# A two-layer mixture of experts on one core: VectorE's word for a count ahead of two weight conversions, and ten operations of the experts' order behind the second pair of tiles

## The chip, the cores and the metric

The kernel runs on one core of one Trainium2 chip. A core has five engines that run their own instruction streams: TensorE (PE in the profile), VectorE (DVE), ScalarE (ACT), GpSimd (POOL) and SyncE (SP), which here issues nearly all transfers. They meet through semaphores. The metric is the time of one execution on the device, in microseconds (us); less is better.

## The reference

The input is q, k, v for 8 batches, 8 heads, 576 positions of width 64. A retention (a causal attention with a decay for each head instead of a softmax) gives a matrix x of 4608 tokens by 512. Two mixture-of-experts layers follow, each with 8 experts and one expert for each token:

```
logits = x @ w_gate                      # layer 2: + modality_bias[modality_id]
e_idx  = argmax(logits, axis=1)          # one expert of 8 for each token
gate_w = softmax(logits)[e_idx]
for e in range(8):
    h        = max(x[mask_e] @ w1[e], 0) # 512 -> 1024
    out[mask_e] = gate_w * (h @ w2[e])   # 1024 -> 512; layer 1: * sigmoid(x @ w_output_gate)[e]
```

The output is the second layer's out, 4608 by 512, in float32.

## The kernel before, in words

**Stages.** In the first 190 us the attention is computed, each token is routed, and its row is scattered to the place of its expert in a buffer in DRAM (xs1). Then come 16 positions: position P_ 0 to 7 is an expert of layer 1, 8 to 15 one of layer 2 (E is 8). Layer 1's results go through the second gate on the way and are scattered to a second buffer (xs2), sorted by their next expert. The experts of layer 2 are taken in an order by size, which is not known before the tokens of layer 1 are counted.

**A position.** An expert's tokens are worked in pairs of tiles of 128 (a pair is 256 rows, `unit(P_, 0, PAIR)` and `unit(P_, 1, PAIR)`), and what is left over in a third block of 128 rows or fewer (`unit(P_, 2, FULL)`). In this run position 6 has two pairs and a third block. In a unit TensorE first makes four quarters of the hidden layer (lines 999 to 1001). ScalarE writes the maximum with zero in float16 (L1101) and VectorE what float16 left out of it (L1213); both are needed by the second product (lines 1007 to 1009), first for the tile b=0, then for b=1. ScalarE and VectorE then cut each result tile to a row of the next layer (`back`, lines 1086 and 1177), the last operation being an x2row.

**Routing of results lags behind.** The rows of a finished unit are transposed by SyncE (x2T, L806), in `turn_next`, which stands in SyncE's `unit` for the unit after next: the rows of the second pair of expert 6 are turned in SyncE's unit for the first pair of expert 7, behind the transpose of that pair's own rows (xT, L820). TensorE makes their second-layer logits (L977, in `logits`) between its other matmuls one unit later than the unit that made them: those of the second pair of expert 6, tile 0, in the middle of the third block's second product. VectorE chooses the expert (`choose`), TensorE counts the rank (`ranks`, L982), VectorE makes the place (`place`), GpSimd scatters.

**Weights.** SyncE loads the next expert's weights in four quarters of 1 MB (stg, L791, `next_w`); ScalarE (L1078) and VectorE (`conv`, L1145) convert a quarter each to two float16 parts. VectorE does two of these conversions at the end of a first pair (line 1222), one in the second pair, one at its end. The slot of a quarter is free again (stg_free) after VectorE's conversion.

**The order of layer 2.** At the end of the first pair of position 6 (`asked`, line 744: P_ is E-2, slot 0), VectorE gives the word `cnt_ask`. TensorE's `counts` (L986) takes it, and with it pr_free1, the slot that VectorE's `place` frees, at the end of its unit, and sums the counts of the eight experts over the partitions (L988). VectorE's `order` (L1237) takes the result (cnt_full), subtracts, and makes the order by ten more operations on 8 or 64 elements of one partition. It ends with four words: ord_sp, ord_pe, ord_ac and ord_po. TensorE, ScalarE and GpSimd take theirs ahead of position 7. SyncE takes ord_sp in `next_w` (line 795) ahead of the first load of position 8's weights, and it issues that load at the end of position 6 (line 924), behind all of position 6's transfers and ahead of all of position 7's. SyncE's instructions, like those of the other engines, run in program order, so what stands behind a wait waits too.

All operations of VectorE's chains go through a helper and so carry its line, L477; they are told apart by their tiles (r_cf is the subtraction's result, wb a converted weight, oh the chosen expert, x2row a result's row).

Of the kernel before, what the change touches and what calls it, by code (L numbers as in the profile page):

```python
# [20 lines left out]
D, F, E = 512, 1024, 8  # L21
# [470 lines left out]
def experts(nc, st, I, K, out):  # L492
# [37 lines left out]
    T = Take(nc)  # L530
# [5 lines left out]
    def cols(P_, w):  # L536

        return slice(0, w) if w != SMALL or P_ < E else slice(P - w, P)
# [26 lines left out]
    def when(eng, reg, op, val):  # L565
        return eng.If_cmp(reg, val, f"IS_{op}")
# [48 lines left out]
    def entered(eng, R_, P_):  # L615

        if P_ < E + 2:
            return ExitStack()
        return when(eng, R_["left"][P_ - E], "GT", 0)
# [24 lines left out]
    def pairs_from(eng, R_, P_, unit, k):  # L644

        pairs, i = R_["np"][P_ % E], R_["i"]
        eng.reg_mov(i, k)
        with eng.While(lambda: eng.snap(i) < eng.snap(pairs)):
            unit(P_, 0, PAIR, True)
            eng.reg_add(i, i, 1)  # L650
            with eng.If(eng.snap(i) < eng.snap(pairs)):
                unit(P_, 1, PAIR, True)
                eng.reg_add(i, i, 1)

    def walk(co, R_, P_, unit, none=None, conv=None, first=None):

        eng, pairs, od = co.eng, R_["np"][P_ % E], R_["od"][P_ % E]
        if P_ < E:
            block, after = co.label("block"), co.label("after")

            def without():
                if none:
                    none()
                if first and P_ == 0:
                    first()
                for q in range(2 if conv and P_ == 0 else 0):
                    conv(0, 2 + q)
                if conv:
                    for slot in range(2):
                        for q in range(2):  # L670
                            brought(eng, R_, P_, conv, slot, q)

            def other():
                with when(eng, pairs, "GT", 1):
                    unit(P_, 1, PAIR, True, 1)
                    pairs_from(eng, R_, P_, unit, 2)
                if conv:
                    with eng.Else():
                        for q in range(2):
                            brought(eng, R_, P_, conv, 1, q)  # L680
            co.unlikely(pairs, "LT", 1, without, block)
            unit(P_, 0, PAIR, False, 0)
            co.unlikely(pairs, "NE", 2, other, block)
            unit(P_, 1, PAIR, True, 1)
            co.to(block)
            co.jump(od, "EQ", 0, after)
            unit(P_, 2, FULL, False)
            co.to(after)
            return
        with when(eng, pairs, "GT", 0):  # L690
            unit(P_, 0, PAIR, False, 0)
            with when(eng, pairs, "GT", 1):
                unit(P_, 1, PAIR, True, 1)
                pairs_from(eng, R_, P_, unit, 2)
        if none:
            with eng.Else():
                none()
        with when(eng, od, "EQ", 2):
            unit(P_, 2, FULL, False)
        with eng.Else():  # L700
            with when(eng, od, "EQ", 1):
                unit(P_, 2, SMALL, False)
        if conv:
            rest(eng, R_, P_, conv)

    def brought(eng, R_, P_, conv, slot, q):

        if P_ + 1 < NP and None not in (slot, q):
            with entered(eng, R_, P_ + 1):
                conv(P_ + 1, 2 * slot + q)  # L710

    def rest(eng, R_, P_, conv):

        with when(eng, R_["np"][P_ % E], "LT", 2):
            with when(eng, R_["np"][P_ % E], "LT", 1):
                for q in range(2):
                    brought(eng, R_, P_, conv, 0, q)
            for q in range(2):
                brought(eng, R_, P_, conv, 1, q)
# [13 lines left out]
    def behind(P_, slot):  # L733

        return P_ < E and (P_, slot) != (0, 0)
# [8 lines left out]
    def asked(P_, slot):  # L744

        return P_ == E - 2 and slot == 0
# [16 lines left out]
    with nc.Block() as block:  # L763
# [374 lines left out]
        def _(ve):  # L1138
            ch = Chain(ve, T, "dve")
            tt, ts, stt, tr = ve.tensor_tensor, ve.tensor_scalar, ve.scalar_tensor_tensor, ve.tensor_reduce  # L1140
            with ExitStack() as rs:
                R_ = registers(rs, ve, "ve", ("i", "was", "early"))
# [63 lines left out]
                def unit(P_, s, w, sure, slot=None, routing=None):  # L1206
                    cs = cols(P_, w)
                    for g in range(4):
                        routes = routing or behind(P_, slot)
                        if routes and g < 3:  # L1210
                            routed(ve, was, s, sure, g, choose, 2)
                        take(ve, "hh_full")
                        stt(hT[:, 1, 2 * g:2 * g + 2, cs], ph[g][:, :, cs], 0.0, hT[:, 0, 2 * g:2 * g + 2, cs], op0=ALU.max, op1=ALU.subtract).then_inc(T["h_full"])  # L1213
                        if routes:
                            if g == 3:
                                routed(ve, was, s, sure, g, choose, 2)
                            routed(ve, was, s, sure, g, place, 2)
                        if P_ == 0 and slot == 0 and g < 2:
                            conv(0, 2 + g)
                        if slot == 1 and g == 1:  # L1220
                            brought(ve, R_, P_, conv, slot, 0)
                    for q in range(2 - (slot or 0)):
                        brought(ve, R_, P_, conv, slot, q + (slot or 0))
                    if routing or asked(P_, slot):
                        ve.sem_inc(T["cnt_ask"])
                    for b in range(blocks[s]):
                        back(s, b) if P_ < E else final(s, b)
                    if asked(P_, slot):
                        order()
                    if P_ < E:  # L1230
                        note(ve, was, s, sure)
# [2 lines left out]
                over = lambda a: a.unsqueeze(1).to_broadcast([1, E, E])  # L1234
                along = lambda a: a.unsqueeze(2).to_broadcast([1, E, E])

                def order():  # L1237

                    take(ve, "cnt_full")
                    ch(tt, r8["cf"], pk[0:1], col("eP")[0:1], op=ALU.subtract)  # L1240
                    ch.tell("pr_free1")
                    ch(stt, r8["key"], r8["cf"], 8.0, col("desc")[0:1], op0=ALU.mult, op1=ALU.add)
                    ch(tt, r64["cmp"], over(r8["key"]), along(r8["key"]), op=ALU.is_gt)
                    ch(tr, r8["rank"], r64["cmp"], axis=AX.X, op=ALU.add)
                    ch(tt, r64["sel"], over(r8["rank"]), along(e8), op=ALU.is_equal)
                    ch(tt, r64["t"], r64["sel"], over(e8), op=ALU.mult)
                    ch(tr, r8["ord"], r64["t"], axis=AX.X, op=ALU.add)
                    ch(ve.tensor_copy, reg2[:, 0:8], r8["ord"])
                    ch(ts, reg2[:, 32:40], r8["ord"], -1.0, E - 1.0, dep=False, op0=ALU.mult, op1=ALU.add)
                    ch(tr, r8["n2"][:, 0:1], r8["cf"], dep=False, axis=AX.X, op=ALU.max)  # L1250
                    ch(ts, reg2[:, 40:41], r8["n2"][:, 0:1], float(EP * PAIR), None, op0=ALU.is_ge)
                    ch.tell("ord_sp", "ord_pe", "ord_ac", "ord_po")
                    ch.end()
# [27 lines left out]
                co = Course(ve, "ve")  # L1281
# [6 lines left out]
                for P_ in range(NP):  # L1288
                    if P_ == E - 3:
                        ch(ve.tensor_copy, cums, cum)  # L1290
                        ch.end()
                    if P_ == E - 1:
                        learn(ve, R_)
                    if P_ == E:
                        with when(ve, R_["early"], "GT", 0):
                            unit(E, 0, PAIR, False, routing=True)
                            final_counts()
                            unit(E, 1, PAIR, False)
                        with ve.Else():
                            routed(ve, was, 0, False, None, lambda b: (choose(b), place(b)))  # L1300
                            ve.sem_inc(T["cnt_ask"])
                            final_counts()
                        less_early(ve, R_)
                    co.leave(R_, P_)
                    ahead(ve, R_, P_)

                    def none():
                        ve.sem_inc(T["cnt_ask"])
                        order()
                    walk(co, R_, P_, unit, none if P_ == E - 2 else None, conv, nothing)  # L1310
                co.end()

        @block.gpsimd
# [123 lines left out]
```

## Time and profile before

| what | value |
|---|---|
| timed runs | 1017.72, 1019.05, 1019.11 us; median 1019.05 |
| profiled execution, own time | 1011.63 us |
| its span, first to last instruction | 1009.9 us |
| mean granted TensorE clock | 0.986 of full speed |
| bytes moved by DMA | 145.15 MB, mean 144 GB/s |

The profile is of one execution, and the rows below are its. Times in a row are microseconds from the start of the span. A row of a timeline is one instruction, or several alike in sequence (x2): start, duration, engine, line, operation, result<-operands; at the end stands, in brackets, how long the engine was idle before it and what released it (DVEq L465, PEq L465 and the like: the engine's own queue stood at a semaphore wait, which the helper at line 465 issues). Matmuls overlap, so the distance of their starts is what one costs, not its duration. SPq rows are SyncE issuing a transfer; the transfer itself lands later.

### The profile page before, as it was taken

To read this page: it belongs to the slowest core of one execution; us is meant where nothing else is said; L and a number is where in the kernel's file an instruction comes from. 1 tells how busy PE (TensorE), PEld (TensorE's weight loads), DVE (VectorE), ACT (ScalarE), POOL (GpSimd) and SP (SyncE) were. 2 spreads that over 40 slices of the span, in tenths; PEclk is the share of its full clock that TensorE was granted. 3 is DMA by queue.
4 is the path that set the end of the run, shared out by engine and by line. 5 is a ranking of instruction groups with operands and counts; after the bars stand their busy time and mean duration, and the time that the engine had idled before them with its cause. 6 is when DMAs were issued, how large, how long until landed. Compare 5 with 4: busy or idle time off the path is not lost. (4 is left out here: it accounts for less than half of the span.)

```text
span 1009.9 us, 24673 instructions
## 1 busy us (share of the span) xinstructions
PE 972.9 (96%) x8929; PEld 699.1 (69%) x8929; DVE 444.7 (44%) x1395; ACT 352.3 (35%) x693; POOL 232.0 (23%) x301
## 2 busy tenths in 40 slices
PE   8999998499999999999999999999999999999995
PEld 5999997366767677676666667667666667766673
DVE  2566667465655666555656565233111111111111
ACT  3555555352534344444434443133111211111111
POOL 4577666301111121211221121101001101001010
PEclk9999999699999999999999999999999999999998
DMA  8998884587648474839455654551121211122100
GB/s 309 309 315 294 280 305 163 170 243 206 150 140 173 111 201 78 229 77 252 144 146 158 160 149 82 169 120 53 43 63 42 74 34 54 43 52 53 53 31 24
DMA packets 180259, 145.15 MB, mean 144 GB/s; under 512 B 136569, under 2 KB 136733, under 8 KB 180128
## 3 DMA queue, kind: packets, MB, share of 16 engines
q1 hardware_dynamic: 171168, 114.89, 42.3%
q0 software_dynamic: 8960, 28.62, 7.8%
q8 instruction: 70, 1.15, 0.5%
q14 instruction: 61, 0.50, 0.2%
HBM read 80.46 MB, written 33.92 MB: 113 GB/s over the span
## 5 line engine op out<-in xcount | busy, mean ns | idle before, releaser
L999 PE MATMUL ph<-xT,wb 128*128 128x256 f16 (+2 forms) x1344 | 337.2, 262 | 0.1
L1001 PE MATMUL ph<-xT,wb 128*128 128x256 f16 (+2 forms) x1344 | 337.3, 262 | 0.0
L1000 PE MATMUL ph<-xT,wb 128*128 128x256 f16 (+2 forms) x1344 | 337.3, 262 | 0.0
L1213 DVE SCALAR_TENSOR_TENSOR hT<-ph,hT 128x512 f16<-128x512 f32 (+2 forms) x168 | 106.0, 637 | 332.4 <-DVEq L465 331.8
L1009 PE MATMUL py<-wb,hT 128*128 128x512 f16 x608 | 230.4, 379 | 0.0
L1008 PE MATMUL py<-wb,hT 128*128 128x512 f16 x608 | 230.3, 379 | 0.0
L1007 PE MATMUL py<-wb,hT 128*128 128x512 f16 x608 | 230.3, 379 | 0.0
L1101 ACT ACTIVATE hT<-ph 128x512 f16<-128x512 f32 (+2 forms) x168 | 92.4, 551 | 200.7 <-ACTq L465 200.4
L999 PEld LDWEIGHTS ph<-xT,wb 128*128 128x128 f16 x1344 | 131.1, 98 | 16.1 <-issue 0.5
L1000 PEld LDWEIGHTS ph<-xT,wb 128*128 128x128 f16 x1344 | 131.1, 98 | 15.7
L1001 PEld LDWEIGHTS ph<-xT,wb 128*128 128x128 f16 x1344 | 131.1, 98 | 12.4
L1339 POOL DMA_INDIRECT out_dram<-yo,idxo x37 | 36.0, 974 | 335.2 <-POOLq L465 335.2
L1009 PEld LDWEIGHTS py<-wb,hT 128*128 128x128 f16 x608 | 59.4, 98 | 71.8
L1007 PEld LDWEIGHTS py<-wb,hT 128*128 128x128 f16 x608 | 59.3, 98 | 63.4
L1008 PEld LDWEIGHTS py<-wb,hT 128*128 128x128 f16 x608 | 59.4, 98 | 63.2
L1328 POOL TENSOR_SCALAR idx<-v_pos 128x1 int32<-128x1 f32 x39 | 24.4, 625 | 324.9 <-POOLq L465 324.9
L477 DVE SCALAR_TENSOR_TENSOR wb<-stg,wb 128x2048 f16<-128x2048 f32 x38 | 86.9, 2286 | 10.0 <-DVEq L465 9.5
L1095 ACT ACTIVATE yo<-py,v_gcol 128x512 f32<-128x512 f32 x37 | 25.4, 687 | 168.1 <-ACTq L465 168.1
L1078 ACT ACTIVATE wb<-stg 128x2048 f16<-128x2048 f32 x38 | 72.3, 1903 | 1.5 <-ACTq L465 1.3
L1092 ACT ACTIVATE x2row<-py,v_s 128x512 f16<-128x512 f32 x39 | 26.8, 687 | 70.3 <-ACTq L465 70.3
L1332 POOL DMA_INDIRECT xs<-x2row,idx x39 | 42.6, 1093 | 37.8 <-POOLq L465 36.5
L313 ACT ACTIVATE a<-pa 128x512 f32<-128x512 f32 x64 | 34.7, 593 | 38.2 <-PE pa L274 38.0
(152 smaller groups left out, 947.0 us busy)
## 6 DMA issues: line engine op xcount, KB each, us to landing
stg<-in_moe_w_dram SPq DMA_DIRECT2D x38, 1024.0 KB, 7.3
qn<-in_q_dram SPq DMA_DIRECT2D x36, 256.0 KB, 4.1
dkn<-in_dk_dram SPq DMA_DIRECT2D x36, 256.0 KB, 5.1
vn<-in_v_dram SPq DMA_DIRECT2D x36, 256.0 KB, 5.6
kn<-in_k_dram SPq DMA_DIRECT2D x32, 256.0 KB, 5.3
xs<-zero SPq DMA_DIRECT2D x8, 262.0 KB, 2.2
xs<-zero SPq DMA_DIRECT2D x8, 258.0 KB, 3.2
w0s<-in_moe_w_dram SPq DMA_DIRECT2D x8, 256.0 KB, 5.6
```

The lines of the kernel that those rows point to most:

```text
L477: r = fn(*a, **kw).then_inc(self.sem, 1)
L999: pe.matmul(o, w1(P_, 0)[:, c, fs], xT[s][:, c, cs], start=(c == 0), stop=False)
L1000: pe.matmul(o, w1(P_, 0)[:, c, fs], xT[s][:, 4 + c, cs], start=False, stop=False)
L1001: m = pe.matmul(o, w1(P_, 1)[:, c, fs], xT[s][:, c, cs], start=False, stop=(c == 3))
L1007: pe.matmul(py[b], hT[:, 0, f, bs], w2(P_, 0)[:, f, :], start=(f == 0), stop=False)
L1008: pe.matmul(py[b], hT[:, 0, f, bs], w2(P_, 1)[:, f, :], start=False, stop=False)
L1009: m = pe.matmul(py[b], hT[:, 1, f, bs], w2(P_, 0)[:, f, :], start=False, stop=(f == 7))
L1078: ac.activation(wb[P_ % 2][:, 0, 2048 * c:2048 * c + 2048], stg[:, 2048 * c:2048 * c + 2048], AF.Copy, scale=WS).then_inc(T["cv_full"])
L1101: ac.activation(hT[:, 0, 2 * g:2 * g + 2, cs], ph[g][:, :, cs], AF.Relu).then_inc(T["hh_full"])
L1213: stt(hT[:, 1, 2 * g:2 * g + 2, cs], ph[g][:, :, cs], 0.0, hT[:, 0, 2 * g:2 * g + 2, cs], op0=ALU.max, op1=ALU.subtract).then_inc(T["h_full"])
L1332: po.indirect_dma_start(out=xs2, out_offset=bass.IndirectOffsetOnAxis(ap=idx[b], axis=0), in_=x, in_offset=None, bounds_check=E * R - 1, o ...
L1339: po.indirect_dma_start(out=out, out_offset=bass.IndirectOffsetOnAxis(ap=idxo[b], axis=0), in_=yo[b], in_offset=None, bounds_check=N - 1, ...
```

## The change

VectorE's `cnt_ask` in position 6 is given ahead of the two conversions at the end of the first pair instead of behind them. `order` is cut in two: `totals` takes the count, subtracts and frees the slot, where all of `order` stood; the other ten operations and the four words stand at the end of the second pair of the same position. For an expert with one pair or none other branches call them (`late`, `none`); this run doesn't take them.

```diff
+                    if asked(P_, slot):
+                        ve.sem_inc(T["cnt_ask"])
                     for q in range(2 - (slot or 0)):
                         brought(ve, R_, P_, conv, slot, q + (slot or 0))
-                    if routing or asked(P_, slot):
+                    if routing:
                         ve.sem_inc(T["cnt_ask"])
                     for b in range(blocks[s]):
                         back(s, b) if P_ < E else final(s, b)
                     if asked(P_, slot):
+                        totals()
+                    if (P_, slot) == (E - 2, 1):
                         order()
...
-                def order():
+                def totals():
 
                     take(ve, "cnt_full")
                     ch(tt, r8["cf"], pk[0:1], col("eP")[0:1], op=ALU.subtract)
                     ch.tell("pr_free1")
+                    ch.end()
+
+                def order():
+
                     ch(stt, r8["key"], r8["cf"], 8.0, col("desc")[0:1], op0=ALU.mult, op1=ALU.add)
...
                     def none():
                         ve.sem_inc(T["cnt_ask"])
+                        totals()
                         order()
-                    walk(co, R_, P_, unit, none if P_ == E - 2 else None, conv, nothing)
+                    walk(co, R_, P_, unit, none if P_ == E - 2 else None, conv, nothing, order if P_ == E - 2 else None)
```

## Rows read from the trace of the kernel before

**Rows 1.** The page, busy time (share of the span) and instructions of each engine

```profile
PE 972.9 (96%) x8929; PEld 699.1 (69%) x8929; DVE 444.7 (44%) x1395; ACT 352.3 (35%) x693; POOL 232.0 (23%) x301
```

**Rows 2.** TensorE's waits: line, released by: us in total, times, longest us

```profile
PE py L1042 <- issue: 12.9, 1, 12.9
...
PE pr L982 <- PEq L465: 1.8, 1, 1.8
```

**Rows 3.** TensorE's timeline where the first pair of expert 6 ends

```profile
525.59 0.38 PE L1009 MATMUL py<-wb,hT 128*128 128x512 f16 x1
527.41 0.17 PE L988 MATMUL pr<-cums,ones 128*128 128x8 f16 x1 [1.44 <-PEq L465]
527.68 0.27 PE L999 MATMUL ph<-xT,wb 128*128 128x256 f16 x1
```

**Rows 4.** VectorE's timeline from the first pair's last rank to the second pair's end

```profile
521.03 0.16 DVE L477 TENSOR_TENSOR cum<-cum,oh 128x8 f16<-128x8 f16 x1
...
524.44 2.29 DVE L477 SCALAR_TENSOR_TENSOR wb<-stg,wb 128x2048 f16<-128x2048 f32 x1 [0.48 <-DVEq L465]
...
533.09 0.15 DVE L477 TENSOR_TENSOR r_cf<-pr,cst 1x8 f32<-1x8 f32 x1 [0.59 <-DVEq L465]
...
535.14 0.14 DVE L477 TENSOR_SCALAR reg<-r_n 1x1 int32<-1x1 f32 x1
...
536.14 1.29 DVE L1213 SCALAR_TENSOR_TENSOR hT<-ph,hT 128x512 f16<-128x512 f32 x2 [0.86 <-DVEq L465]
...
541.37 0.29 DVE L477 TENSOR_SCALAR oh<-w_w,v_m,cur 128x8 f16<-128x8 f32 x1
...
553.83 0.74 DVE L477 SCALAR_TENSOR_TENSOR x2row<-py,v_s,x2row 128x512 f16<-128x512 f32 x1
```

**Rows 5.** TensorE's timeline, the first rank matmul in the second pair

```profile
541.86 0.17 PE L982 MATMUL pr<-oh,tri 128*128 128x8 f16 x1 [1.85 <-PEq L465]
```

**Rows 6.** TensorE's timeline, third block of expert 6 and expert 7's first matmul

```profile
551.15 0.22 PE L999 MATMUL ph<-xT,wb 128*128 128x128 f16 x1
...
557.81 0.35 PE L977 MATMUL pr<-wg,x2T 128*128 128x24 bf16 x8
...
561.95 0.27 PE L999 MATMUL ph<-xT,wb 128*128 128x256 f16 x1
```

**Rows 7.** SyncE's issues behind expert 6

```profile
534.41 0.37 SPq L824 DMA_DIRECT2D meta<-xs  x1
535.99 1.36 SPq L791 DMA_DIRECT2D stg<-in_moe_w_dram  x2
538.27 4.94 SPq L820 DMA_TRANSPOSE xT<-xs  x1
552.10 3.86 SPq L806 DMA_TRANSPOSE x2T<-x2row  x2
```

**Rows 8.** SyncE's issues: loads, then x2T, shortest and longest case; a row transpose alone

```profile
402.58 1.14 SPq L791 DMA_DIRECT2D stg<-in_moe_w_dram  x2
...
410.78 1.45 SPq L806 DMA_TRANSPOSE x2T<-x2row  x1
...
455.99 0.89 SPq L791 DMA_DIRECT2D stg<-in_moe_w_dram  x2
...
464.61 1.69 SPq L806 DMA_TRANSPOSE x2T<-x2row  x1
...
498.25 2.37 SPq L820 DMA_TRANSPOSE xT<-xs  x1
```

**Rows 9.** x2T transposes issued at 410.78, at 464.61, from 529 to 534: issue to landing

```profile
DMA to landing us min/median/max: 4.1/4.1/4.1
...
DMA to landing us min/median/max: 5.0/5.0/5.0
...
DMA to landing us min/median/max: 2.8/2.8/2.8
```

**Rows 10.** Busy us of each engine (x instructions) where TensorE starts again; then PEclk

```profile
189.50:193.80 4.30, 4.30 (x11) 1.51 (x12) 3.29 (x6) 0.00 (x0) 3.35 (x1) 0.50 0.76 142
```

More of the change, by code (lines that the diff above doesn't have):

```diff
@@ L653, in pairs_from, with walk @@
                 eng.reg_add(i, i, 1)
-    def walk(co, R_, P_, unit, none=None, conv=None, first=None):
+    def walk(co, R_, P_, unit, none=None, conv=None, first=None, late=None):
         eng, pairs, od = co.eng, R_["np"][P_ % E], R_["od"][P_ % E]
@@ L678, in other @@
                     with eng.Else():
+                        if late:
+                            late()
                         for q in range(2):
```

## The prediction

> **What bounds the kernel now.** I read first the page's list of busy times. TensorE is busy 96% of the span and the next engine, VectorE, 44% [rows 1]. So time is won or lost where TensorE stands still. Next I read the list of TensorE's waits. Its longest entry, 12.9 us, is the step from attention to the experts, which the change doesn't touch; the 1.8 us at L982 is in the changed stretch [rows 2]. Third I read the timeline of TensorE there. The first pair of expert 6 ends with the matmul at 525.59; the count (L988) starts only at 527.41 and the second pair at 527.68 [rows 3]. Matmuls of this form start 0.216 us apart, so without a wait the count would start at 525.80 and, at the 0.03 us that such a small matmul takes in the stream, the second pair at 525.83. This wait costs 1.85 us. A second one stands in the second pair: the rank matmul at 541.86 comes after 1.85 us of idle time [rows 5].
>
> Fourth I read VectorE's timeline for what ended these waits [rows 4]. VectorE is through with the first pair's ranks at 521.19 (521.03 + 0.16). Then come two conversions, of which the second ends at 526.73, and only then the word that TensorE's count waits for. The order follows at 533.09: the subtraction, ending at 533.24, and ten operations, ending at 535.28. The next unit's first max starts at 536.14, and everything behind it is late: the choice for the second pair's routing ends at 541.66 (541.37 + 0.29), and the rank matmul starts 0.2 later. So VectorE is what binds TensorE at the second wait.
>
> Last I read SyncE's timeline, because the order's end tells SyncE too (ord_sp) [rows 7]. Its queue is in order. At 534.41 it issues the last transfer of expert 6. Then it takes ord_sp, and the two loads of the next weights leave at 535.99, 0.71 us after the order's last operation. Behind them come, at 538.27, the transpose of expert 7's first rows, and at 552.10 the two transposes of the second pair's results (x2T), which the third block of expert 6 needs for its logits.
>
> **The change, part by part.** *The word ahead of the conversions.* It adds and removes no work. It can go out at 521.2, the slot pr_free1 is given at the same point, and TensorE comes at 525.80; so the first wait goes, 1.85 us. What is late next is the second wait: TensorE would be at the rank matmul at 541.86 - 1.85 - 1.85 = 538.16, and VectorE ends its choice no earlier for this part. Alone it would be worth nothing at the end of the pair.
>
> *Ten operations off the front of the second pair.* The max came 0.86 us after the order's last operation; the subtraction came 0.59 after the operation before it, behind three words and a take [rows 4]. By that gap the max now starts at 533.24 + 0.59 = 533.83 instead of 536.14, 2.3 us earlier, and with it the conversion and the choice. The rank matmul moves to 539.55, still later than 538.16. Both parts together win 2.3 us at the end of the second pair, not 1.85 + 2.3: it ends at 551.15 - 2.3 = 548.85 [rows 6].
>
> *The ten operations behind the second pair.* VectorE's last operation of the pair now ends at 553.83 + 0.74 - 2.3 = 552.27 [rows 4]. After 0.59 the ten follow, 2.04 us (533.24 to 535.28), to 554.9. Two things hang on that.
>
> First, the third block's maxima on VectorE start behind them: at 554.9 + 0.86 = 555.76, and one takes at most 0.65 us (two of the wider form take 1.29). TensorE's second half of that block began at 557.81 - 6 x 0.216 = 556.51 [rows 6] and now waits for the first maximum until some 556.4. So of the 2.3 us this alone gives back all but about 0.1.
>
> Second, and much larger: ord_sp comes at the end of the second pair, and SyncE stands at it from 534.8 on. Queued behind it are the two loads (1 MB each), expert 7's row transpose, the two x2T transposes and a small load. None of these was held before: the order came 0.5 us after SyncE was there. The words to TensorE, ScalarE and GpSimd are taken only in front of expert 7, after 561.95, and 554.9 is early enough for them.
>
> TensorE needs the first x2T for the logits at L977, which ran at 557.81 [rows 6]. The loads now leave at 554.9 + 0.71 = 555.6. From two loads to the landing of an x2T transpose issued behind a row transpose of 256 rows, the trace has four cases; the shortest is 402.58 to 410.78 + 4.1 = 414.88, 12.3 us, the longest 455.99 to 464.61 + 5.0 = 469.61, 13.6 us, the others 12.6 and 12.7 [rows 8, 9]. I take 12.6: the landing is at 568.2. A lower bound comes from this place itself: the row transpose was through SyncE at 538.27 + 4.94 = 543.21, 7.2 us after the loads, then 0.2 to the next issue and the shortest landing, 2.8 us: 10.2, so 565.8 [rows 7, 9]. The logits then run at 568.2 instead of 557.81, 10.4 us late (8.0 to 11.4). What stands between them and expert 7's first matmul (561.95) is 4.1 us of TensorE's own work, unchanged; expert 7's rows land before that (they are ahead of x2T in the queue), the third block's other maxima are done long before, and the two weight quarters, though they leave 20 us later, are also ahead of x2T and are converted only in expert 7's first pair. The 2.3 us won before and the 0.1 of VectorE lie in front of this stall and count for nothing. Behind it TensorE has no idle time that could take it back: [rows 2] has nothing of that size there.
>
> *The clock.* TensorE then stands from about 557 to 568. The one stretch of such idle time that the trace shows, 12.9 us, left the granted clock at 0.50, the lower level of 1.2 GHz, for 4.3 us after the work began again at 189.5 [rows 2, 10]. At half the clock 4.3 us do the work of 2.15, so 2.2 us are lost. I add these 2.2; the ends are 0 (the clock stays up, as it did over the 1.85 us waits) and 4.3 (it stays down for twice as long).
>
> *Sum.* +10.4 + 2.2 = +12.6 us. The profiled execution took 1011.63 us (span 1009.9); its own time would be 1024.2. The median of the three timed runs is 1019.05, 7.4 us more, a difference the trace doesn't explain; the loss is added to it: 1031.6 us.
>
> **A rule weighed.** The row transpose issued at 538.27 behind two loads took 4.94 us of SyncE's time, the one at 498.25 with no load ahead of it 2.37 [rows 7, 8], so here the transposes are held by the loads in front. The Trainium skill, in "DMA: Bandwidth & Descriptors", section "Queues, rings and completion order", says that a DMA engine takes descriptors in the order of its ring, but that a later one can finish before an earlier one, so completions of one issuing engine don't come first in, first out. By that rule the x2T need not wait for the loads to end, which gives a smaller loss; it is the third rival.
>
> **The rivals.** *Faster: the 2.3 us stay.* Place: the x2T transposes. It decides on whether the first of them lands before TensorE is at the logits, some 555.5 at the earliest, 557.8 at the latest. For: all 2.3 us are real on VectorE, and the order's words are wanted at expert 7 only by three of four engines. Against: SyncE is the fourth, and 555.6 is when its loads leave. It also needs the third block's first maxima to be in time. Price -2.3: 1016.7 us.
>
> *Same: the ten operations only change sides.* If SyncE were not held, the third block's wait for its first maximum gives the 2.3 us back, as worked out: -0.1, 1018.9 us. Against it stands the same queue. That the change doesn't do what it says comes to this price too.
>
> *Slower, but less: transposes aren't held by the loads.* Row transpose issued 2.28 after the loads as before (535.99 to 538.27), at 557.9, 2.37 us long as at 498.25, 0.2, then 2.8 to landing: 563.3, a loss of 5.5, with 0 to 2.2 for the clock: 1024.6 to 1026.8 us. For it: the rule above. Against: the four cases in the trace.
>
> **How the numbers follow.** A change of under 0.2%, 2 us, can't be told from none here. The forecast has 0.87, the smaller loss 0.05, faster 0.04, same 0.04. The forecast's own bounds are +8.0 + 0 and +11.4 + 4.3, 1027.1 to 1034.8. For 8 in 10 I give 1025 to 1035.5, which takes in most of the third rival and some of the spread of the runs. Slower: 0.87 + 0.05 = 0.92.
>
> **What would show it.** Right: the count follows the first pair with no idle time; the rank matmul in the second pair about 2.3 us earlier, with some 1.4 us of idle time left; the two loads near 555.6, next to the end of the order; an idle stretch of 10 us or more in TensorE's third block in front of L977, released by an x2T transpose; granted clock 0.5 just behind it. Wrong: L977 in the third block without a wait, or the loads at 536 as before. If the stall is there but the clock stays up, the time is near 1029.

## The result, and the profile after

The changed kernel took 1029.54 us (median of four runs, 1027.03 to 1031.26), the kernel before 1018.96 us (four runs). By the medians it is 10.6 us slower. The ratio as estimated over all runs is 1.0111 (95% interval 1.0090 to 1.0131), which is 11.3 us (9.2 to 13.3). Forecast were 1031.6 us and a loss of 12.6, so the direction and the place were right and the loss was taken 2 us too large.

The two profiles can't be laid over each other as they are: their spans differ by 18.1 us, and 6.7 of these lie ahead of the change. The first list is TensorE's waits in the changed kernel (line, released by: us in total, times, longest us). Its lines stand two further down than those of before: L979, L984, L990, L1001 and L1009 are the L977, L982, L988, L999 and L1007 of before, L1215 is L1213, and SyncE's L808 and L822 are L806 and L820. The kernels of the experiments are shifted by none to three lines.

```profile
PE py L1044 <- issue: 13.0, 1, 13.0
PE pr L979 <- PEq L465: 10.3, 2, 10.1
PE px L338 <- DVE og L331: 4.2, 2, 3.4
...
PE py L1009 <- PEq L465: 1.7, 1, 1.7
```

New are 10.3 us at the logits (L979, 10.1 of them at once) and 1.7 us at L1009, the second product. The two waits of [rows 3, 5] (1.44 at the count, 1.85 at the ranks) are gone from this list or shrunk. The line with L338 stands in the attention, which the change doesn't touch. There TensorE waited 3.4 us once, and the granted clock was at its lower level from 171.2 to 201.9; in the profiled execution of before that was 176.8 to 193.8. So the experts' work began 6.7 us later, for a reason ahead of the change. To compare, I count from VectorE's second conversion in expert 6's first pair, which both kernels do alike: 524.44 before [rows 4], 531.18 after. From it to expert 7's first matmul it is 37.51 us before [rows 6] and 48.61 after: 11.1 us more.

VectorE in the changed kernel, from that conversion to the third block (the rows that answer to rows 4; start, duration, what):

```profile
531.18 2.29 DVE L477 SCALAR_TENSOR_TENSOR wb<-stg,wb 128x2048 f16<-128x2048 f32 x1 [0.48 <-DVEq L465]
...
539.71 0.16 DVE L477 TENSOR_TENSOR r_cf<-pr,cst 1x8 f32<-1x8 f32 x1 [0.59 <-DVEq L465]
540.40 1.29 DVE L1215 SCALAR_TENSOR_TENSOR hT<-ph,hT 128x512 f16<-128x512 f32 x2 [0.53 <-DVEq L465]
...
558.18 0.74 DVE L477 SCALAR_TENSOR_TENSOR x2row<-py,v_s,x2row 128x512 f16<-128x512 f32 x1
559.41 0.15 DVE L477 SCALAR_TENSOR_TENSOR r_key<-r_cf,cst 1x8 f32<-1x8 f32 x1 [0.49 <-DVEq L488]
...
561.15 0.14 DVE L477 TENSOR_SCALAR reg<-r_n 1x1 int32<-1x1 f32 x1
562.08 0.42 DVE L1215 SCALAR_TENSOR_TENSOR hT<-ph,hT 128x256 f16<-128x256 f32 x1 [0.79 <-DVEq L465]
```

The first max of the second pair comes 0.69 us behind the subtraction's start, where it was 3.05. The ten operations stand at 559.41 to 561.29, between the pair's last x2row and the third block's first max.

SyncE (answers to rows 7):

```profile
541.03 0.74 SPq L826 DMA_DIRECT2D meta<-xs  x1
562.01 1.36 SPq L793 DMA_DIRECT2D stg<-in_moe_w_dram  x2
564.29 5.79 SPq L822 DMA_TRANSPOSE xT<-xs  x1
570.57 2.63 SPq L808 DMA_TRANSPOSE x2T<-x2row  x2
```

It was through with the small load at 541.77 and stood until the two weight loads left at 562.01, 0.72 us after VectorE's last operation. In the kernel before it stood there for about a microsecond. Only then came the row transpose (5.79 us) and the x2T.

TensorE (answers to rows 3, 5 and 6):

```profile
532.45 0.17 PE L990 MATMUL pr<-cums,ones 128*128 128x8 f16 x1
532.48 0.27 PE L1001 MATMUL ph<-xT,wb 128*128 128x256 f16 x1
...
546.12 0.17 PE L984 MATMUL pr<-oh,tri 128*128 128x8 f16 x1 [0.79 <-PEq L465]
...
562.65 0.38 PE L1009 MATMUL py<-wb,hT 128*128 128x512 f16 x1 [1.66 <-PEq L465]
...
574.16 0.37 PE L979 MATMUL pr<-wg,x2T 128*128 128x24 bf16 x8 [10.06 <-PEq L465]
...
579.79 0.27 PE L1001 MATMUL ph<-xT,wb 128*128 128x256 f16 x1
```

The count has no wait, and the second pair begins 0.03 us behind it. The rank matmul waits 0.79 us. The third block waits 1.66 us for VectorE's first max and then 10.06 us for x2T. From the logits to expert 7's first matmul it is 5.63 us, before 4.14 [rows 6]. Why, the clock shows (busy us of each engine with its instructions in brackets, TensorE first; then the granted clock, the DMA share and GB/s):

```profile
567.20:574.10 6.90, 0.00 (x0) 0.00 (x0) 0.00 (x0) 0.00 (x0) 0.00 (x0) 0.50 1.07 245
574.20:577.30 3.10, 3.10 (x15) 1.19 (x16) 1.41 (x7) 0.60 (x3) 0.00 (x0) 0.50 0.70 143
577.40:579.70 2.30, 2.30 (x12) 1.04 (x11) 0.00 (x0) 0.00 (x0) 0.00 (x0) 1.00 0.27 59
```

In these last 6.9 us of the stall no engine computes and the DMA engines are busy throughout. The clock went to 0.50 in the stall and stayed there for 3.2 us behind it. The record of its semaphore in the trace has the first x2T landed at 573.88, 11.87 us behind the loads, and the logits start 0.28 us later. In the kernel before it landed at 555.8 (issued at 552.10 [rows 7], 3.7 us to landing), 2.0 us ahead of the logits: this path had little to spare.

### The profile page after: what moved, and what is told of

Read it like the earlier page. It is cut to its first block, busy times and chain, and to the rows that moved or that the text cites. A ratio compares the mean times of both kernels' runs of the same rounds, so it can differ in the third digit from the quotient of the medians.

```text
span 1028.0 us, 24674 instructions
## 1 busy us (share of the span) xinstructions
PE 978.1 (95%) x8929; PEld 702.9 (68%) x8929; DVE 445.4 (43%) x1395; ACT 351.5 (34%) x693; POOL 231.5 (23%) x301
## 5 line engine op out<-in xcount | busy, mean ns | idle before, releaser
L1001 PE MATMUL ph<-xT,wb 128*128 128x256 f16 (+2 forms) x1344 | 337.5, 262 | 0.0
L1215 DVE SCALAR_TENSOR_TENSOR hT<-ph,hT 128x512 f16<-128x512 f32 (+2 forms) x168 | 105.8, 637 | 332.9 <-DVEq L465 330.2
L1009 PE MATMUL py<-wb,hT 128*128 128x512 f16 x608 | 231.0, 380 | 1.7 <-PEq L465 1.7
L1001 PEld LDWEIGHTS ph<-xT,wb 128*128 128x128 f16 x1344 | 131.2, 98 | 16.1 <-issue 0.3
L1009 PEld LDWEIGHTS py<-wb,hT 128*128 128x128 f16 x608 | 59.4, 98 | 65.6 <-issue 2.4
L477 DVE SCALAR_TENSOR_TENSOR wb<-stg,wb 128x2048 f16<-128x2048 f32 x38 | 86.9, 2287 | 10.1 <-DVEq L465 10.1
L177 POOL DMA_INDIRECT xs<-xr,pi x36 | 40.6, 1128 | 32.9 <-DVE xr L233 15.9
```

Of the source, the lines that this page charges most:

```text
L177: nc.gpsimd.indirect_dma_start(out=rows[x.row], out_offset=bass.IndirectOffsetOnAxis(ap=gr.pi[:, t:t + 1], axis=0), in_=gr.xrow[:, t, :], ...
L477: r = fn(*a, **kw).then_inc(self.sem, 1)
L1001: pe.matmul(o, w1(P_, 0)[:, c, fs], xT[s][:, c, cs], start=(c == 0), stop=False)
L1009: pe.matmul(py[b], hT[:, 0, f, bs], w2(P_, 0)[:, f, :], start=(f == 0), stop=False)
```

## The experiments

The theory: SyncE's queue, held by ord_sp, makes the loss; VectorE, not the count, binds the second pair. The rivals: the early count, VectorE's ten operations in front of the third block, or the loads alone. The first four ran on one chip, where the kernel before took 1013.15 us (21 runs), the other three on another, where it took 1018.39 (12 runs). The absolute times in the first expectations were made for 1019, so what is to be compared is the difference. The chip shows in the attention too: in the four traces of the first chip TensorE's longest wait at L338 is 0.8 us and VectorE's second conversion starts at 522.56 to 525.03, as in the profile of before (524.44); in the three of the second chip it is 3.3 us and 529.66 to 531.37, as in the profile after (531.18).

**The word alone.** The order stays whole behind the first pair.

```diff
                     if asked(P_, slot):
                         totals()
-                    if (P_, slot) == (E - 2, 1):
                         order()
```

> The word ahead of the conversions alone; the whole order stands behind the first pair as before. Theory (SyncE's queue behind ord_sp makes the loss; VectorE binds the second pair): the count's wait of 1.85 us goes, the rank matmul's wait grows from 1.85 to 3.7 us, nothing is won: 1019.0 us (1018.5 to 1019.3). Rival (each wait of TensorE counts by itself): -1.85 us, 1017.1. Rival (the early count is what made the kernel slower): near 1029.

Measured: 1012.48 us against 1013.15, ratio 0.9996 (0.9987 to 1.0006), no difference. TensorE's first rank matmul in the second pair, and the clock around it:

```profile
540.60 0.17 PE L984 MATMUL pr<-oh,tri 128*128 128x8 f16 x1 [3.31 <-PEq L465]
```

```profile
537.00:540.60 3.60, 0.29 (x2) 0.03 (x1) 2.62 (x7) 0.81 (x4) 0.00 (x0) 1.00 1.01 408
541.00:544.30 3.30, 3.30 (x9) 1.17 (x8) 2.52 (x12) 0.59 (x3) 1.32 (x3) 0.50 0.90 236
```

The wait at the count is gone and that at the ranks has grown from 1.85 to 3.31 us. One wait of 3.3 us in place of two of under 1.9 left the clock at 0.50 for 3.4 us in this execution. From the second conversion to expert 7 this trace has 39.18 us against 37.51 before, 1.7 more, which is what 3.4 us at half the clock would cost by an estimate; the timed runs show no such loss. So the word ahead isn't worth its 1.85 us, as forecast.

**The ten operations alone.** The word stays behind the conversions.

```diff
-                    if asked(P_, slot):
-                        ve.sem_inc(T["cnt_ask"])
...
-                    if routing:
+                    if routing or asked(P_, slot):
                         ve.sem_inc(T["cnt_ask"])
```

> The ten operations behind the second pair alone; the word stays behind the two conversions. Theory: VectorE is as early as with both parts, so the loads leave at the same time, and the whole loss is there: 1029.5 us (1028.5 to 1030.5), with the count's wait of some 1.6 us back and hidden in front of the stall. Rival (the early count made it slower): 1019. Rival (both parts add to the loss): between 1020 and 1028.

Measured: 1024.13 us, 11.0 more than before, ratio 1.0113 (1.0098 to 1.0128), the same as with both parts. TensorE's logits in the third block:

```profile
568.15 0.37 PE L979 MATMUL pr<-wg,x2T 128*128 128x24 bf16 x8 [9.92 <-PEq L465]
```

The stall is the same to 0.2 us, and the way from the second conversion to expert 7 is 48.60 us against 48.61. The loss belongs to the moved operations, and the early count has no part in it.

**The loads behind the transposes.** Both parts as in the changed kernel; SyncE takes ord_sp and loads position 8's first two quarters behind expert 7's rows and the x2T.

```diff
                         def early_w():
-                            if 1 < P_ < E - 1:
+                            if 1 < P_ < E:
                                 next_w(P_ + 1, 0)
+                            if P_ == E - 1:
+                                learn(sp, R_)
...
-                        if P_ >= E - 2:
+                        if P_ >= E - 1:
                             next_w(P_ + 2, 0)
```

(`learn` reads what the order wrote, so it moves along.)

> Both parts as in the changed kernel, and SyncE takes ord_sp and issues the two loads for position 8 behind expert 7's first rows and the second pair's x2T instead of in front of them. Theory: x2T lands as early as before the change, the 10 us stall and the low clock go; 2.4 us won in the second pair, of which the third block's wait for its first maximum (1.66 us in the changed kernel) gives back most: 1018.3 us (1017.8 to 1019.0). Rival (VectorE's ten operations in front of the third block make the loss): stays near 1029. Rival (the loads are then too late for their conversion in expert 7's first pair): 1020 to 1025, with waits there.

Measured: 1011.59 us, 1.6 less than before, ratio 0.9983 (0.9974 to 0.9992). SyncE, and TensorE's second product of the third block:

```profile
536.30 1.98 SPq L822 DMA_TRANSPOSE xT<-xs  x1
550.21 3.85 SPq L808 DMA_TRANSPOSE x2T<-x2row  x2
...
555.76 1.42 SPq L793 DMA_DIRECT2D stg<-in_moe_w_dram  x2
```

```profile
556.41 0.38 PE L1009 MATMUL py<-wb,hT 128*128 128x512 f16 x1 [1.63 <-PEq L465]
```

The x2T leaves at 550.21, as soon as its rows are there, and the loads 5.5 us later. No wait at the third block's logits is left. With the queue freed, VectorE's operations are as in the changed kernel, with the same 1.6 us in front of the second product: the ten operations there cost 1.6 us, not 10. And the loads weren't too late: expert 7's first pair takes 21.34 us, before 21.33. From the second conversion to expert 7 the trace has 36.81 us, 0.7 less than before; the timed gain is larger, and its interval (0.8 to 2.6 us) just excludes that. It is also more than was expected (0 to 1.2 us); what the rest comes from is open.

**The wait alone.** SyncE takes ord_sp where the changed kernel does, but issues the loads behind the transposes.

```diff
-                        if P_ >= E - 2:
-                            next_w(P_ + 2, 0)
+                        if P_ == E - 2:
+                            take(sp, "ord_sp")
+                        else:
+                            if P_ >= E - 1:
+                                next_w(P_ + 2, 0)
```

(`early_w` loads for position 8 as above, and `next_w` no longer takes the word itself.)

> Both parts as in the changed kernel; SyncE takes ord_sp where it did, but issues the two loads behind expert 7's first rows and x2T. So the late word still holds the transposes, and the loads no longer do. Theory: the row transpose leaves at the word, takes 2.4 us instead of 5.8, x2T lands some 3 us behind it: logits 4 to 5 us late, with 0 to 1.5 us for the clock: 1023.5 us (1022.9 to 1025.5). Rival (the loads in front don't hold transposes, the word alone does): near 1029. Rival (only the loads hold them): 1018.3.

Measured: 1018.24 us, 5.1 more than before, ratio 1.0052 (1.0038 to 1.0065). SyncE, then TensorE, then the stretch behind the logits:

```profile
553.65 2.08 SPq L820 DMA_TRANSPOSE xT<-xs  x1
556.21 2.60 SPq L806 DMA_TRANSPOSE x2T<-x2row  x2
```

```profile
559.79 0.35 PE L980 MATMUL pr<-wg,x2T 128*128 128x24 bf16 x8 [4.39 <-PEq L465]
```

```profile
560.80:564.20 3.40, 3.40 (x9) 1.18 (x8) 0.96 (x5) 0.60 (x3) 0.00 (x0) 0.50 0.79 264
```

The row transpose took 2.08 us of SyncE's time with no load ahead of it; with two loads ahead, in the changed kernel, 5.79. The stall is 4.39 us instead of 10.06, and the logits come 37.23 us behind the second conversion, 3.9 later than before; the rest of the loss lies behind them, where the last row has the clock at 0.50 for 3.4 us. So the late word holds the transposes for some 4 us, and the loads in front of them for nearly 6 more.

**Only SyncE's word late.** The kernel before, with one word moved (its order is two chains instead of one, which makes it 0.1 us longer): the order tells TensorE, ScalarE and GpSimd where it did, and SyncE at the end of the second pair.

```diff
-                    ch.tell("ord_sp", "ord_pe", "ord_ac", "ord_po")
+                    ch.tell("ord_pe", "ord_ac", "ord_po")
...
                     if (P_, slot) == (E - 2, 1):
+                        ve.sem_inc(T["ord_sp"])
```

> The kernel before, with all of its order where it stood and the word behind the conversions; only the word to SyncE (ord_sp) is given at the end of the second pair. No operation of VectorE moves but this word. Theory: the loads leave 0.6 us behind the end of the second pair's last x2row, the x2T 12 us later, TensorE waits some 10 us in the third block: the whole loss, +11 us on the kernel before (10 to 12.5). Rival (VectorE's moved operations make part of the loss): +6 or less.

Measured: 1030.52 us against 1018.39, 12.1 more, ratio 1.0112 (1.0093 to 1.0130). SyncE's two loads, TensorE's logits in the third block, and the clock in the second pair:

```profile
562.66 1.36 SPq L793 DMA_DIRECT2D stg<-in_moe_w_dram  x2
```

```profile
574.08 0.37 PE L979 MATMUL pr<-wg,x2T 128*128 128x24 bf16 x8 [9.19 <-PEq L465]
```

```profile
548.40:551.70 3.30, 3.30 (x9) 1.12 (x8) 2.05 (x8) 0.60 (x3) 1.39 (x3) 0.50 0.08 31
```

One semaphore, with no work moved, makes the whole loss (11.4 us by the ratio; 13.3 in this trace, from the second conversion to expert 7). In this execution the clock fell also behind the ranks' wait of 1.82 us; in the profiled execution of before it stayed up behind the same wait.

**TensorE kept at work in the stall.** The changed kernel with 44 matmuls between the first two parts of the third block's second product.

```diff
                         second(0, (2 * q, 2 * q + 1))
+                        if (P_, s, q) == (E - 2, 2, 0):
+                            for n in range(44):
+                                pe.matmul(ph[0].rearrange("p a b -> p (a b)"), K["ones"], K["ones"].unsqueeze(1).to_broadcast([P, 4, P]), start=True, stop=True)
```

> The changed kernel with 44 matmuls of 512 columns (some 9.5 us) by which TensorE fills the stall in the third block, between the first two parts of the second product; their result is not used. Theory (the low clock behind the stall costs 1.5 us): the granted clock stays at 1.00, and the logits of the third block stand 4.1 us ahead of expert 7's first matmul instead of 5.6: +9.3 us on the kernel before instead of +11 (8.5 to 10). Rival (the clock costs nothing that counts): +10.6 to +11.2. Rival (the matmuls last longer than the stall): over +11.2.

Measured: 1026.78 us, 8.4 more than before, ratio 1.0080 (1.0065 to 1.0096). The stretch of the 44 matmuls and that behind it, up to expert 7's first matmul:

```profile
564.20:574.50 10.30, 9.52 (x45) 4.12 (x42) 0.00 (x0) 0.00 (x0) 0.00 (x0) 1.00 1.07 284
574.60:578.70 4.10, 4.09 (x27) 1.97 (x28) 1.41 (x7) 0.60 (x3) 0.00 (x0) 1.00 0.75 149
```

The clock stayed at 1.00, and the stretch behind the logits took 4.1 us again: 1.5 us of the loss is the clock's. The logits themselves came 0.3 us later than in the changed kernel, so that the way from the second conversion to expert 7 is 1.2 us shorter (47.37 us against 48.61). The timed loss of 8.4 us lies just below what was expected (8.5 to 10); the difference of the two timed losses, 10.6 - 8.4 = 2.2 us, agrees with the trace only within their intervals.

**The order early.** The kernel before, with the count and the whole order at the beginning of expert 6: TensorE counts behind the first quarter of its first pair, VectorE does the order in front of that pair's first max, and the word that the counts are ready stands where they are copied, at the start of position 5.

```diff
                     if P_ == E - 3:
                         ch(ve.tensor_copy, cums, cum)
                         ch.end()
+                        ve.sem_inc(T["cnt_ask"])
...
                         quarter(g)
+                        if asked(P_, slot) and g == 0:
+                            counts(cums)
                         route(g)
...
                     cs = cols(P_, w)
+                    if asked(P_, slot):
+                        order()
                     for g in range(4):
```

> The kernel before, with the count and the whole order moved forward: VectorE's word stands behind the copy of the counts that position 5 begins with, TensorE counts behind the first quarter of expert 6's first pair, VectorE does the order in front of that pair's first max, where it was idle for 2.1 us. Theory: both waits of TensorE go (1.85 us each), the second down to some 0.5 us, and the third block has nothing in front of its maxima: -3.1 us on the kernel before (-2.5 to -3.7). Rival (only the count's wait is won, the rest returns in the third block as in the changed kernel): -0.5 to -1.9. Rival (the order in front of the first pair delays its choice and ranks): 0 or slower.

Measured: 1014.56 us against 1018.39, 3.8 less, ratio 0.9964 (0.9950 to 0.9978): faster than both kernels. By the trace, from expert 6's first matmul to expert 7's, it is 54.78 us against 57.49, 2.7 less, which lies inside the interval (2.2 to 5.1). TensorE's first rank matmul in the second pair, and VectorE's order:

```profile
544.36 0.17 PE L982 MATMUL pr<-oh,tri 128*128 128x8 f16 x1 [0.42 <-PEq L465]
```

```profile
515.45 0.15 DVE L477 TENSOR_TENSOR r_cf<-pr,cst 1x8 f32<-1x8 f32 x1 [2.34 <-DVEq L465]
...
518.56 0.69 DVE L1215 SCALAR_TENSOR_TENSOR hT<-ph,hT 128x512 f16<-128x512 f32 x1 [0.92 <-DVEq L465]
```

The order takes more than the gap of 2.1 us that was there: VectorE waits 2.34 us for the count, and the first max starts 8.90 us behind the pair's first matmul, where it was 5.59. But VectorE has made these 3.3 us up by its second conversion (20.00 us behind that matmul, 19.98 before). The rank matmul waits 0.42 us instead of 1.85, the count not at all, and nothing stands in front of the third block.

## Why the prediction was right, and where it was off

*The word ahead, worth nothing alone:* shown by the word alone (0.9996).

*Second pair 2.3 us earlier:* from the second conversion to the ranks it was 17.42 us before [rows 4, 5] and 14.94 after, 2.5 us earlier. The wait left there was put at 1.4 us and was 0.79 at the ranks with 0.25 at the logits before them, which came a little late.

*The third block's wait, 2.3 us given back but for 0.1:* mis-sized. It was 1.66 us, since the order ended 0.35 us sooner than in the sum (30.11 us behind the second conversion, 30.46 worked out), the max came 0.79 us behind it and was 0.42 us long where 0.65 was the bound. This part and the one before it together are a small gain: 1.6 us in the kernel with the loads behind the transposes, 0.7 by its trace.

*SyncE held by ord_sp:* shown from both sides. Late word without any moved work: the whole loss. Moved work without the held transposes: no loss.

*Logits 10.4 us late:* 9.6 after (42.98 us behind the second conversion, 33.37 before). The loads left 0.3 us sooner than worked out, by the same landmark (30.83 us behind the conversion, 31.16 in the sum), and the logits came 12.15 us behind them, where I took 12.6 to the landing: the shortest of the four cases, 12.3, was nearer than their middle. The trace has a fifth case that was passed over, loads at 227.55 and an x2T issued at 237.79 and landed 3.1 us later, 13.3 us in all, inside the range of the four. The step from a neighbouring place in the trace was sound; its middle was not better than its end.

*The clock, 2.2 us:* the right cause, mis-sized; it was 1.5. I took the 4.3 us at the lower level from the one long idle stretch of before; here it was 3.2 us. The kernel with TensorE kept at work shows that this term is the clock's.

*Transposes not held by the loads (the third rival):* the Trainium skill, "DMA: Bandwidth & Descriptors", section "Queues, rings and completion order", says that completions of one issuing engine don't come first in, first out. No run here shows that for these transposes: SyncE needed 5.79 us to issue one behind two loads and 2.08 with none ahead, and by the semaphores' records in the trace of the changed kernel the landings come in the order of issue (second load 570.22, row transpose 572.26, first x2T 573.88).

*Faster, same:* neither came, because the fourth engine did want its word early, as the text against them said. What they would have been can be seen in the kernel with the loads behind: 1.6 us gained, between their 2.3 and 0.1.

By the trace the sum is 9.6 + 1.5 = 11.1 us, against 12.6 forecast; the timed loss is 10.6 by the medians and 9.2 to 13.3 by the ratio's interval, which doesn't tell the two apart. The 7.4 us by which the profiled execution of before ran under the median have their like in the 6.7 us that the two profiles differ by ahead of the change, and in the seven traces of the experiments that difference goes with the chip, as do the 5.2 us between the medians of the kernel before. So the profile of before and its timed runs probably came from two chips. Which chip they ran on is not on record, and what differs between the chips stays open.

## What to carry to other kernels

A word that is given at the end of a chain has a reader on every engine that takes it, and the reader that matters is the one with an in-order queue behind its wait: follow what stands behind that wait, not what the word is for. Work off the critical engine should go where that engine can make the time up before another needs its result: the count and the order in front of the first pair were worth 3.8 us (2.7 by the trace), the order behind the second pair cost 10.6. And where two waits follow each other, taking the first away is worth nothing if the second is bound by another engine.

## What the runs showed of the hardware

With two loads of 1 MB just ahead in the queue SyncE needed 5.79 us for one row transpose of 256 rows (the changed kernel), with none ahead 2.08 (the wait alone). In the first layer of the trace of before those issued within 2.4 us of two such loads took 4.94 to 7.07 us, one issued 6.2 us behind them 2.78, and those with no such load in the 9 us before them 1.87 to 2.37.

The granted clock fell to 0.50, for about 3.4 us, behind single waits of 3.31 us (the word alone) and 4.39 us (the wait alone), and once behind one of 1.82 us (only SyncE's word late), where a wait of 1.85 us in the execution of before left it at 1.00. At half the clock 3.4 us would cost 1.7, an estimate. By the traces such short waits can cost more than their length, and not in every execution.
